# Attention and mixture of experts on one core: the first k and q in two pieces, constants later, products without use at the start, and another order of the attention part

## The chip, the core and the metric

The kernel runs on one NeuronCore of a Trainium2 chip. A core has five engines, each with a queue of its own that it works off in order: PE (TensorE, matrix products, with weight loads that overlap them, PEld), DVE (VectorE), ACT (ScalarE), POOL (GpSimd) and SP (SyncE, which here issues nearly all DMA transfers). Products are written to PSUM, eight banks of 512 float32 a partition, from where ACT or DVE copy them to the core's main memory (SBUF). The metric is the time of one execution in device microseconds; smaller is better.

## The reference

Block-causal attention over 8 batches of 8 heads (576 positions, 64 columns a head, blocks of 64), and behind it a layer of 8 experts, to each of which 576 of the 4608 tokens are assigned greedily by their logits:

```python
scores = scale * np.matmul(q, k.transpose(0, 1, 3, 2))
mask = block_i >= block_j
scores = np.where(mask, scores, -1000000000.0)
attn = np.exp(scores - np.max(scores, axis=-1, keepdims=True))
attn = attn / (np.sum(attn, axis=-1, keepdims=True) + 1e-09)
return np.matmul(attn, v).astype(np.float32)
...
logits = x @ w_gate
order = np.argsort(-logits.flatten())   # greedy, at most N // E tokens an expert
...
for e in range(E):
    h = np.maximum(x[assigned == e] @ w1[e], 0.0)
    out[assigned == e] = h @ w2[e]
```

## The kernel before

The kernel has two stages. The first is attention with the logits (class `Attn`), the second routing and experts (class `Moe`).

Attention works on 32 steps n; a step holds two heads (one in rows 0 to 63 and one in rows 64 to 127), and two steps form a pair u, whose q and k are loaded together. Each float32 q and k is split into two float16 parts (`split`): a cast gives the high part (L277 or L279, on ACT, DVE or POOL), a subtraction the low part (L286). The parts are transposed, for the first four steps on PE (L298, with copies out of PSUM at L306), later by DMA transposes that SP issues (L323), into `qT` and `kT`. `swap` (L336) copies the lower half of kT into the upper half of `kS`, so that two products per block (with kT and with kS) give the scores (L357). A step's scores come in three groups of block rows. For each group DVE finds the row maxima (L375), scales them (L379), and ACT writes the exponentials P (L383). P is transposed on PE with an identity matrix (L427): 25 blocks of 128 x 128 a step, in seven tiles of one PSUM bank each (four blocks, the last one block), in the order of the table PTO; ACT or DVE copies each tile into PT (L408, L410). The value products (L474) read PT and V; DVE scales their result (L444), the result is split again (L454, L458 and L410), and with it the logits are formed (L514) and the rows for the experts are written to device memory (L494, L499). Scores and value products write 64 columns of PE's array, transposes and logits 128; the kernel's own plan calls these shapes N and W.

What sets the order: every task is a Python generator that names its engine (or a choice of engines, as 'AGD'), an estimated duration and the events it needs. `Sched.run` plans with these numbers, picks the next task by start and priority, and writes the instructions of each engine in that order. So a change in a duration, a bias, a priority (the table `PR`, the names PE, PVE, PF) or a limit changes the order of the whole attention stage. Two score buffers ('S', two banks each) and four single banks ('x') are handed out in the plan. Bank 3 is not handed out; products without use write to it.

At the start, `gate` loads w_gate (L227) and scales it, `consts` makes constants for the second stage (L594 to L606 on POOL and DVE), among them the float16 identity `idh` (L598). The first k and q are split in whole halves of nine blocks (step n = 0), four products without use (L283, L301) stand in front and behind the first transposes.

Of the kernel before, what the change touches and what calls it, by code (L numbers as in the profile page):

```python
# [9 lines left out]
F16 = mybir.dt.float16  # L10
# [9 lines left out]
class Sched:  # L20
# [65 lines left out]
    def start(s, k, eng):  # L86
# [73 lines left out]
class Attn:  # L160
# [63 lines left out]
    def gate(s):  # L224
        nc, sc = s.nc, s.sc
        yield S, 25, 'hw'
        nc.sync.dma_start(out=s.wf, in_=s.wg.rearrange("(c p) e -> p c e", p=P))  # L227
        sc.dma(224, ('wg', 0))
        yield D, 100, ('wg', 0)
# [35 lines left out]

    def split(s, nm):
# [3 lines left out]
        for n in range(s.N):  # L270
            u, i = n // 2, n % 2
            yield 'AGD', (573, 760, 760), s.BH, ('ld', nm, n), ('idh', 0), ('tr', nm, 2 * (u - s.NQ) + 1)
# [7 lines left out]
            if n == 0:  # L280

                for _ in range(s.NWU[nm == 'q']):
                    nc.tensor.matmul(s.psb[:, 3], lhsT=s.moe.idh, rhs=b[:, 0:8, hi], start=True, stop=True)  # L283
                sc.free[T] = max(sc.free[T], sc.now) + 427 * s.NWU[nm == 'q']
            yield ('GD', (1300, 780), s.BL) if n else (D, 669)
# [4 lines left out]
            if n < s.NPE:  # L290
                if i == 0:
                    t = s.d[nm + 'T', u] = s.wp.tile([P, 18, P], F16, tag=nm + 'T', name=f"{nm}T{u}", bufs=s.TB)
                yield T, 9 * 107, ('idh', 0), 'x'
# [21 lines left out]
                sc.add(ev(A, 0, 5, ps[0], h=h), 0, sc.now + 200)  # L315
                sc.add(ev(D, 5, 9, ps[1], h=h), 0, sc.now + 200)
# [13 lines left out]
    def swap(s):  # L330

        nc, sc = s.nc, s.sc
        for n in range(s.N):
            u, i = n // 2, n % 2
            yield 'DG', (560, 1280), s.BK, ('tr', 'k', n), ('s', 2 * (u - s.TB) + 1)
            (nc.vector if sc.eng == D else nc.gpsimd).tensor_copy(s.kS[u % s.TB][64:, 9 * i:9 * i + 9], s.d['kT', u][:64, 9 * i:9 * i + 9])  # L336
# [754 lines left out]
```

## Time and profile before

| | us |
|---|---|
| median of 3 runs | 781.56 (781.21 to 783.07) |
| the profiled execution | 781.08 |
| its span, first to last instruction | 779.3 |
| PE busy in the span | 709.6 (91%) |
| DVE busy | 572.2 (73%) |
| ACT busy | 523.3 (67%) |
| POOL busy | 366.1 (47%) |

Engines overlap, so the busy times do not add up to the span. A row of the profile names the source line, the engine, the operation and the tiles; "idle before" is the time its engine waited ahead of it, and the name behind the arrow is what ended that wait. The granted clock (PEclk) is the share of TensorE's full clock.

### The profile page before, as it was taken

How to read it: one execution, taken by the hardware profiler on the slowest of the kernel's cores; microseconds unless marked ns; L12 is line 12 of the kernel's file. 1: busy time of each engine (PE TensorE's matmuls, PEld its weight loads, DVE VectorE, ACT ScalarE, POOL GpSimd, SP SyncE). 2: the span in 40 equal slices, each digit the busy share in tenths (PEclk: the TensorE clock that was granted, in tenths of full speed). 3: DMA queues.
4: the chain of work that ended last, by engine and by line, in shares of the span. 5: the costliest groups of instructions: out<-in, count | busy, mean ns of one | idle time of the engine just before them, and what ended most of it. 6: DMA issues, size and time to landing. Idle time of an engine off the chain costs nothing.

```text
span 779.3 us, 18377 instructions
## 1 busy us (share of the span) xinstructions
PE 709.6 (91%) x6329; PEld 456.0 (59%) x6329; DVE 572.2 (73%) x2299; ACT 523.3 (67%) x1411; POOL 366.1 (47%) x431
## 2 busy tenths in 40 slices
PE   5999999998999999237998999999999999899995
PEld 3676666666677667116546647557475475574752
DVE  6989898888899888887988969778686783520210
ACT  5999987987887876337658497684957847292210
POOL 6785452727263562103244175481944808764001
PEclk9999999999999999658999999999999999999998
DMA  9999999999999997425054192774918439851001
GB/s 194 189 202 187 220 191 193 207 198 221 189 223 169 235 179 188 118 101 178 2 180 159 42 302 58 248 146 149 223 35 254 126 142 236 250 131 42 21 26 36
DMA packets 273485, 124.42 MB, mean 160 GB/s; under 512 B 247280, under 2 KB 256496, under 8 KB 273392
## 3 DMA queue, kind: packets, MB, share of 16 engines
q1 hardware_dynamic: 267504, 104.37, 62.2%
q0 software_dynamic: 5888, 18.88, 7.9%
q8 instruction: 49, 0.80, 0.4%
q14 instruction: 44, 0.36, 0.2%
HBM read 71.32 MB, written 18.87 MB: 116 GB/s over the span
## 4 chain that ended last, share of the span: by engine, by line
PE 75%; DVE 11%; ACT 6%; DMA 4%; issue 3%; POOL 1%; another core or an unknown queue 0%; POOLq 0%; DVEq 0%; SPq 0%; ACTq 0%
PE h L995 23%; PE y L1020 15%; PE psb L427 11%; PE psb L474 10%; PE psb L357 10%; PE y L1024 2%; DVE jk L741 1%; DMA qT<-q 1%; ACT W L914 1%; DVE m L375 1%; ACT raw L910 1%; ACT ja L715 1%; ACT P L383 1%; DVE h L835 1%; DMA kT<-k 1%
## 5 line engine op out<-in xcount | busy, mean ns | idle before, releaser
L995 PE MATMUL h<-X,W 128*128 128x320 f16 (+3 forms) x1536 | 195.5, 287 | 0.3 <-issue 0.3
L995 PEld LDWEIGHTS <-W 128*128 128x128 f16 x1536 | 142.1, 98 | 43.5 <-issue 4.1
L383 ACT ACTIVATE P<-psb,m 128x576 f32<-128x576 f32 (+8 forms) x288 | 149.9, 553 | 22.3 <-DVE m L379 20.5
L1020 PE MATMUL y<-W,HH 128*128 128x512 f16 x512 | 152.2, 379 | 0.0
L375 DVE TENSOR_REDUCE m<-psb 128x1 f32<-128x576 f32 (+8 forms) x288 | 124.6, 480 | 17.0 <-PE psb L357 16.3
L916 POOL TENSOR_TENSOR W<-raw,W 128x1024 f16<-128x1024 f32 x56 | 118.4, 2135 | 37.9 <-ACT W L914 33.4
L427 PE MATMUL psb<-mident,P 128*128 128x128 f32 x800 | 107.6, 280 | 5.5 <-DVE Xf L444 1.7
L474 PE MATMUL psb<-PT,V 128*64 128x448 f32 (+5 forms) x784 | 99.9, 390 | 1.4 <-ACT PT L408 0.7
L981 ACT ACTIVATE HH<-h 128x320 f16<-128x320 f32 (+3 forms) x128 | 52.3, 411 | 70.1 <-PE h L995 61.8
L427 PEld LDWEIGHTS psb<-mident,P 128*128 128x128 f32 x800 | 86.1, 141 | 21.7 <-issue 4.9
L1020 PE MATMUL y<-W,HL 128*128 128x512 f16 x256 | 97.0, 379 | 0.0
L1011 POOL DMA_INDIRECT out_dram<-yo,ix x40 | 39.1, 978 | 118.8 <-ACT yo L1003 86.7
L408 ACT ACTIVATE PT<-psb 128x512 f32<-128x512 f32 (+1 forms) x159 | 81.1, 576 | 15.2 <-PE psb L427 13.6
L357 PE MATMUL psb<-kT,qT 128*64 128x512 f16 (+7 forms) x640 | 86.2, 295 | 2.8 <-DMA qT<-q 2.5
L983 DVE SCALAR_TENSOR_TENSOR HL<-h,HH 128x320 f16<-128x320 f32 (+3 forms) x128 | 56.7, 452 | 43.5 <-ACT HH L981 36.7
L945 POOL DMA_INDIRECT xg<-x,ix x40 | 40.3, 1007 | 98.0 <-DVE ix L883 68.8
L357 PEld LDWEIGHTS <-qT 128*64 128x64 f16 x1280 | 61.3, 111 | 41.1 <-issue 17.6
L357 PE MATMUL psb<-kS,qT 128*64 128x512 f16 (+7 forms) x640 | 78.0, 291 | 0.0
L1020 PEld LDWEIGHTS <-HH 128*128 128x128 f16 x512 | 46.9, 98 | 51.4 <-issue 1.0
L910 ACT ACTIVATE raw<-raw 128x512 f32<-128x512 f32 x112 | 67.7, 627 | 5.7 <-DMA raw<-in_moe_w_dram 5.6
L474 PEld LDWEIGHTS psb<-PT,V 128*64 128x64 f32 x784 | 47.5, 138 | 36.6 <-issue 24.1
L914 ACT ACTIVATE W<-raw 128x512 f16<-128x512 f32 x112 | 68.6, 629 | 0.0
(203 smaller groups left out, 1065.6 us busy)
## 6 DMA issues: line engine op xcount, KB each, us to landing
raw<-in_moe_w_dram SPq DMA_DIRECT2D x64, 512.0 KB
x<-XR SPq DMA_DIRECT2D x8, 1152.0 KB
kn<-in_k_dram SPq DMA_DIRECT2D x15, 576.0 KB
qn<-in_q_dram SPq DMA_DIRECT2D x15, 576.0 KB
V<-in_v_dram SPq DMA_DIRECT2D x64, 128.0 KB
V<-in_v_dram SPq DMA_DIRECT2D x16, 64.0 KB
xg<-x,ix POOLq DMA_INDIRECT x40
out_dram<-yo,ix POOLq DMA_INDIRECT x40
```

The source lines that it names most:

```text
L357: nc.tensor.matmul(ps[64 * h:64 * h + 64, o + a:o + e], lhsT=A[:, h, 64 * i:64 * i + 64], rhs=K[:, h, a:e], start=st, stop=not st)
L375: nc.vector.tensor_reduce(m[:, 0, c:c + 1], ps[:, o:o + 64 * (i + 1)], axis=AX.X, op=OP.max)
L383: nc.scalar.activation(Pt[:, s.OFF[i]:s.OFF[i] + 64 * (i + 1)], ps[:, o:o + 64 * (i + 1)], AF.Exp, bias=m[:, 1, c:c + 1], scale=s.ESC, acc ...
L408: s.nc.scalar.activation(out, in_, AF.Copy)
L427: nc.tensor.transpose(ps[:, a], s.Pb[n % s.NP][:, s.OFF[i] + 128 * j:s.OFF[i] + 128 * j + P], s.ident)
L474: nc.tensor.matmul(ps[64 * h:64 * h + 64, 64 * (i0 - b0):64 * (b1 - b0)], lhsT=vn[:, j, 2 * (n % 2) + h, :], rhs=pt[:, s.PTI[(j, i0)]:s.PT ...
L910: nc.scalar.activation(raw[:,x],raw[:,x],AF.Copy,scale=s.WS)
L914: nc.scalar.activation(hi[:,x],raw[:,x],AF.Copy)
L916: nc.gpsimd.tensor_tensor(lw,raw,hi,op=OP.subtract)
L983: nc.vector.scalar_tensor_tensor(HL[:,f,ts],ps,0.0,HH[:,f,ts],op0=OP.max,op1=OP.subtract)
L995: nc.tensor.matmul(ps,lhsT=W[:,a,d,f*P:f*P+P],rhs=X[:,4*(d//2)+d%2+l,ts],start=(d==0 and n==0),stop=(d==3 and n==2))
L1020: if m<4: nc.tensor.matmul(ps,lhsT=Z[:,f,m*P:m*P+P],rhs=Y[:,a,f],start=(f==n==0),stop=(f==7 and n==2))
```

## The change

The change has these parts:

- The first q and k (step 0) are split in two pieces of five and four blocks (`piece`, new): ACT casts the five, DVE the four, DVE subtracts both; each piece is transposed by itself into one bank. k's upper copy `kS` is written from PSUM by ACT (`twin`, new), no longer from kT by `swap`; kT's pieces and q's second piece are copied by DVE, q's first piece by ACT.
- The load of w_gate stands behind the first loads of k and q; the gate's scaling and the constants on DVE wait, in the plan, for the swap of step 1 (the event `('sw', 1)`). `idh` is made by POOL behind the identity.
- Products without use (`warm`): six at the very front, which read only `idh`, and one behind each of the four pieces' transposes, for the four before.
- Loads get a limit: a load is issued only when the plan holds at most so much transfer time ahead (QL 3000, QV 1000, QW 2500).
- Swaps may also run on ACT; biases, priorities and planner settings are other numbers, and the tiles of P are transposed in ascending order.

```diff
+            if e == 'xx':
+                if len(s.res['x']) < 2:
+                    return None
+                t = max(t, sorted(s.res['x'].values())[1])
+                continue
...
+            if isinstance(e, tuple) and e[0] == 'q':
+                t = max(t, s.q - e[1])
                 continue
...
+        s.sc.free[G] = 5600
...
-        yield S, 25, 'hw'
+        yield S, 25, 'hw', ('gl', 0)
         nc.sync.dma_start(out=s.wf, in_=s.wg.rearrange("(c p) e -> p c e", p=P))
         sc.dma(224, ('wg', 0))
-        yield D, 100, ('wg', 0)
+        yield D, 100, ('wg', 0), ('sw', 1)
...
+    def warm(s, k):
+        for _ in range(k):
+            s.nc.tensor.matmul(s.psb[:, 3], lhsT=s.moe.idh, rhs=s.moe.idh[:, None, :].to_broadcast([P, 4, P]), start=True, stop=True)
+
+    def piece(s, nm, hi, t2, t, c0, c1, e, h):
...
+        yield e, (95 + .835 * w if e == A else 69 + .52 * w), ('ld', nm, 0), ('idh', 0)
...
+        yield D, 69 + 1.042 * w
+        nc.vector.tensor_tensor(b[:, :, 1 - hi], a, b[:, :, hi], op=OP.subtract)
...
+        yield T, 75 * (c1 - c0), 'x'
...
+        for c in range(c0, c1):
+            nc.tensor.transpose(ps[:, c - c0], t2[:, c].rearrange("p a d -> p (a d)"), s.moe.idh)
+        s.warm(s.NW1)
...
+        yield (D, 51 + 83 * (c1 - c0)) if k or c0 else (A, 51 + 110 * (c1 - c0))
...
+    def twin(s, ps, c0, c1, tk, h):
+        yield A, 51 + 110 * (c1 - c0)
+        s.nc.scalar.activation(s.kS[0][64:, c0:c1], ps[:64, :c1 - c0], AF.Copy)
...
+                for c0, c1, e in ((0, 5, A), (5, 9, D)):
+                    sc.add(s.piece(nm, hi, t2, t, c0, c1, e, h), s.PR['split'], sc.now)
...
-            yield 'DG', (560, 1280), s.BK, ('tr', 'k', n), ('s', 2 * (u - s.TB) + 1)
+            yield 'DAG', (560, 1010, 1280), s.BK, ('tr', 'k', n), ('s', 2 * (u - s.TB) + 1)
...
-    PE = 4
-    PVE = 1
+    PE = 2
+    PVE = 2
...
-    BH = 300.0
+    BH = -300.0
...
-    BV = -150.0
+    BV = 150.0
...
-    PTO = (6, 5, 4, 3, 2, 1, 0)
+    PTO = (0, 1, 2, 3, 4, 5, 6)
...
-    PR = dict(load_qk=9, load_v=6, split=3, swap=1, scores=5, transpose=3, values=6, rows=7, logits=5, gate=1)
+    QW = 2500
+    QV = 1000
+    QL = 3000
+    PX = 2
+    PR = dict(load_qk=9, load_v=6, split=3, swap=1, scores=3, transpose=3, values=8, rows=7, logits=5, gate=1)
...
+        s.warm(s.NW0)
+        sc.free[T] = 2000 + 427 * s.NW0
...
+        s.idh=s.cp.tile([P,P],F16,name="m_idh"); nc.gpsimd.tensor_copy(s.idh,s.ident); sc.set(('idh',0))
...
-        yield D,700
-        s.idh=cp.tile([P,P],F16,name="m_idh"); nc.vector.tensor_copy(s.idh,s.ident); s.sc.set(('idh',0))
+        yield D,900,('sw',1)
...
-            sc.ST = 500
+            sc.ST = 100
...
-            sc.KEEP = 0
-            sc.MARGIN = 100
+            sc.MARGIN = 0
+            sc.KEEP = 1
```

DVE at the start of the program, before (the last rows of the constants, the gate, then the first k and q; in these rows `k`, `q` are the split halves, `kn`, `qn` the loaded ones):

```order
L604 TENSOR_SCALAR m_i_136<-m_it 128x32
L605 TENSOR_SCALAR m_b_140<-m_i_136 128x32 x2
L606 TENSOR_SCALAR m_io_144<-m_fi 128x3
L230 TENSOR_SCALAR wgs<-wf 128x4x8
L232 SCALAR_TENSOR_TENSOR wgs<-wf,wgs 128x4x8
L286 TENSOR_TENSOR k_0_156<-kn_128,k_0_156 128x9x64
L286 TENSOR_TENSOR q_0_162<-qn_146,q_0_162 128x9x64
L306 COPY kT_161<-psb 128x512
L336 COPY kS_114<-kT_161 64x1152
L306 COPY qT_166<-psb 128x512
L375 TENSOR_REDUCE m_209<-psb 128x1 x2
```

and the same place now, from its second row on:

```order
L289 CAST k_0_125<-kn_133 128x4x64
L291 TENSOR_TENSOR k_0_125<-kn_133,k_0_125 128x4x64
L291 TENSOR_TENSOR k_0_125<-kn_133,k_0_125 128x5x64
L289 CAST q_0_123<-qn_135 128x4x64
L309 COPY kT_126<-psb 128x512
L291 TENSOR_TENSOR q_0_123<-qn_135,q_0_123 128x5x64
L291 TENSOR_TENSOR q_0_123<-qn_135,q_0_123 128x4x64
L309 COPY kT_126<-psb 128x640
L347 CAST k_0_125<-kn_133 128x9x64
L309 COPY qT_124<-psb 128x512
L347 CAST q_0_123<-qn_135 128x9x64
L442 TENSOR_REDUCE m_201<-psb 128x1 x2
```

The constants and the gate have left this place; pieces of k and q stand there, the copy into kS is gone, and casts of the second halves (step 1, nine blocks) have come in, one of them ahead of qT's copy.

ACT at the same place, before:

```order
L277 ACTIVATE k_0_156<-kn_128 128x9x64
L277 ACTIVATE q_0_162<-qn_146 128x9x64
L306 ACTIVATE kT_161<-psb 128x640
L306 ACTIVATE qT_166<-psb 128x640
L277 ACTIVATE q_0_162<-qn_146 128x9x64
L383 ACTIVATE P_88,m_209<-psb,m_209 128x576
```

and now:

```order
L287 ACTIVATE k_0_125<-kn_133 128x5x64
L287 ACTIVATE q_0_123<-qn_135 128x5x64
L323 ACTIVATE kS_116<-psb 64x512
L323 ACTIVATE kS_116<-psb 64x640
L307 ACTIVATE qT_124<-psb 128x640
L450 ACTIVATE P_90,m_201<-psb,m_201 128x576
```

The two copies into kS have come in, and the cast of q's second half has gone to DVE.

PE in the steady part, before, around one run of transposes of P (`mident` is the identity, `P_88` a step's exponentials); two places 33 rows apart:

```order
L357 LDWEIGHTS qT_584
L357 MATMUL psb<-kS_114,qT_584 64x128
L427 MATMUL psb<-mident,P_88 128x128 x16
L357 LDWEIGHTS qT_584
L357 MATMUL psb<-kT_497,qT_584 64x320
```

```order
L357 MATMUL psb<-kS_114,qT_584 64x64
L427 MATMUL psb<-mident,P_88 128x128 x4
L474 MATMUL psb<-PT_106,V_109 64x448 x4
L357 LDWEIGHTS qT_584
L357 MATMUL psb<-kT_497,qT_584 64x512
```

and one now:

```order
L541 MATMUL psb<-PT_108,V_110 64x64 x2
L541 MATMUL psb<-PT_109,V_110 64x128 x2
L494 MATMUL psb<-mident,P_102 128x128 x25
L422 LDWEIGHTS qT_634
L422 MATMUL psb<-kT_560,qT_634 64x512
```

Before, a step's 25 transposes stand in several runs between scores and value products; now all 25 stand in one, with products of 64 columns on both sides.

More of the change, by code (lines that the diff above doesn't have):

```diff
@@ L247, in load_qk @@
                     sc.dma(1450 * step, ('ld', nm, 2 * u + i))
-                    if u:
+                    if u == i == 0 and nm == 'q':
+                        sc.set(('gl', 0))
+                    if step == 2:
                         sc.ev['ld', nm, 2 * u + 1] = sc.ev['ld', nm, 2 * u]
@@ L264, in load_v, with out @@
             sc.dma(320, ('ld', 'v', u), 625)
+    def warm(s, k):
+        for _ in range(k):
+            s.nc.tensor.matmul(s.psb[:, 3], lhsT=s.moe.idh, rhs=s.moe.idh[:, None, :].to_broadcast([P, 4, P]), start=True, stop=True)
+    def piece(s, nm, hi, t2, t, c0, c1, e, h):
+        nc, sc = s.nc, s.sc
+        w = 64 * (c1 - c0)
+        yield e, (95 + .835 * w if e == A else 69 + .52 * w), ('ld', nm, 0), ('idh', 0)
+        a, b = s.d[nm, 0][:, c0:c1], t2[:, c0:c1]
+        if e == A:
+            nc.scalar.activation(b[:, :, hi], a, AF.Copy)
+        else:
+            nc.vector.tensor_copy(b[:, :, hi], a)
+        yield D, 69 + 1.042 * w
+        nc.vector.tensor_tensor(b[:, :, 1 - hi], a, b[:, :, hi], op=OP.subtract)
+        h.append(-1)
+        if len(h) == 2:
+            sc.set(('sp', nm, 0))
+        yield T, 75 * (c1 - c0), 'x'
+        tk = sc.acq('x')
+        ps = s.bank(tk).bitcast(F16).rearrange("p (c t) -> p c t", t=P)
+        for c in range(c0, c1):
+            nc.tensor.transpose(ps[:, c - c0], t2[:, c].rearrange("p a d -> p (a d)"), s.moe.idh)
+        s.warm(s.NW1)
+        sc.free[T] = max(sc.free[T], sc.now) + 213 * s.NW1
+        k = nm == 'k'
+        if k:
+            sc.add(s.twin(ps, c0, c1, tk, h), s.PR['split'], sc.now + 200)
+        yield (D, 51 + 83 * (c1 - c0)) if k or c0 else (A, 51 + 110 * (c1 - c0))
+        if sc.eng == A:
+            nc.scalar.activation(t[:, c0:c1], ps[:, :c1 - c0], AF.Copy)
+        else:
+            nc.vector.tensor_copy(t[:, c0:c1], ps[:, :c1 - c0])
+        s.out(nm, h, tk)
+    def out(s, nm, h, tk):
+        h.append(tk)
+        if nm == 'q' or h.count(tk) == 2:
+            s.sc.rel('x', tk)
+        if len(h) == (6 if nm == 'k' else 4):
+            s.sc.set(('tr', nm, 0))
+            if nm == 'k':
+                s.sc.set(('sw', 0))
+    def twin(s, ps, c0, c1, tk, h):
+        yield A, 51 + 110 * (c1 - c0)
+        s.nc.scalar.activation(s.kS[0][64:, c0:c1], ps[:64, :c1 - c0], AF.Copy)
+        s.out('k', h, tk)
     def split(s, nm):
@@ L279, in split @@
                 (nc.vector if sc.eng == D else nc.gpsimd).tensor_copy(b[:, :, hi], a)
[L280 to L285, printed above, removed]
+            yield 'GD', (1300, 780), s.BL
             (nc.vector if sc.eng == D else nc.gpsimd).tensor_tensor(b[:, :, 1 - hi], a, b[:, :, hi], op=OP.subtract)
@@ L314, in split @@
                     sc.ev['ti', u] = sc.now
-                sc.add(ev(A, 0, 5, ps[0], h=h), 0, sc.now + 200)
-                sc.add(ev(D, 5, 9, ps[1], h=h), 0, sc.now + 200)
+                sc.add(ev(A, 0, 5, ps[0], h=h), s.PX, sc.now + 200)
+                sc.add(ev(D, 5, 9, ps[1], h=h), s.PX, sc.now + 200)
                 continue
@@ L361, in scores @@
                     sc.set(('s', n))
+                if n == 0:
+                    sc.ev['s1', 0] = sc.now
                 sc.add(s.softmax(n, g, tk, ps), s.PS, sc.now + 200)
@@ L557 @@
     PL = 6
-    PF = 3
+    PF = 5
     NPE = 4
```

36 lines of the change are left out of this document (25 added, 11 removed).

## The prediction

> **What bounds the kernel now.** I read the windows first (per stretch: busy time and count of each engine, granted clock, share of the DMA engines), then the timeline of the first 14 us, then places of PE's timeline, then the groups and the waits.
>
> ```profile
> core 0: us, PE busy (x) PEld busy (x) DVE busy (x) ACT busy (x) POOL busy (x), PEclk, DMA share, GB/s
> 31.00:314.00 283.00, 276.12 (x3016) 191.02 (x3013) 249.55 (x785) 236.42 (x735) 142.00 (x226) 0.99 1.07 200
> 110.00:120.00 10.00, 8.68 (x119) 6.23 (x119) 8.47 (x24) 6.28 (x20) 6.80 (x9) 0.83 1.03 177
> 190.00:200.00 10.00, 7.91 (x73) 5.00 (x74) 6.92 (x23) 4.02 (x13) 5.54 (x5) 0.83 0.94 186
> 314.00:779.30 465.30, 412.68 (x3110) 251.36 (x3110) 298.39 (x1448) 265.54 (x621) 200.46 (x142) 0.95 0.46 133
> ```
>
> Attention ends near 314 us. In its steady part PE is busy 276 of 283 us, DVE 250, ACT 236. The 465 us behind it (routing and experts) hold the same instructions in the same order on every engine in both kernels, so I take them as they are. The whole change is therefore decided ahead of 314 us: before the first scores, and in how PE's stream of scores (L357), transposes of P (L427) and value products (L474) is packed.
>
> **Term 1, the start.** Rows of the timeline: start, duration, what; in brackets the idle time before and who ended it.
>
> ```profile
> 0.73 0.46 SPq L227 DMA_DIRECT2D wf<-in_moe_w_gate_dram  x1
> 1.25 0.49 SPq L245 DMA_DIRECT2D kn<-in_k_dram  x1
> 4.84 0.68 ACT L277 ACTIVATE k<-kn 128x576 f16<-128x576 f32 x1 [2.84 <-DMA kn<-in_k_dram]
> 5.76 0.25 DVE L599 TENSOR_SCALAR m_tri<-m_it 128x128 f16<-128x128 int32 x1 [3.11 <-POOL m_it L594]
> 6.18 0.68 ACT L277 ACTIVATE q<-qn 128x576 f16<-128x576 f32 x1 [0.65 <-DMA qn<-in_q_dram]
> 7.28 0.75 DVE L286 TENSOR_TENSOR k<-kn,k 128x576 f16<-128x576 f32 x1
> 7.57 0.98 POOL L279 CAST k<-kn 128x576 f16<-128x576 f32 x1 [1.53 <-DMA kn<-in_k_dram]
> 7.94 1.22 DVE L286 TENSOR_TENSOR q<-qn,q 128x576 f16<-128x576 f32 x1
> 8.08 1.14 PE L298 MATMUL psb<-m_idh,k 128*128 128x128 f16 x9 [0.59 <-DVE k L286]
> 9.26 0.43 DVE L306 COPY kT<-psb 128x512 f16<-128x512 f16 x1
> 10.64 0.42 DVE L306 COPY qT<-psb 128x512 f16<-128x512 f16 x1
> 11.12 0.20 PEld L357 LDWEIGHTS <-qT 128*64 128x64 f16 x4 [0.28 <-DVE qT L306]
> 12.66 1.29 DVE L375 TENSOR_REDUCE m<-psb 128x1 f32<-128x576 f32 x2 [1.59 <-PE psb L357]
> 13.42 0.68 PE L298 MATMUL psb<-m_idh,k 128*128 128x128 f16 x9
> ...
> L410 DVE CAST XT<-Xf 128x576 f16<-128x576 f32 (+2 forms) x28 | 14.4, 516 | 0.2
> ```
>
> k's high half is cast by 5.52, but its low half starts at 7.28: DVE works through the constants and the gate in between, and those waited for POOL. In the new order they stand later, and k's transfer is issued first. Following DVE's new rows: k is there at 4.84 - 0.52 (issue 0.73 for 1.25) = 4.32, q at 5.66. Cast of four blocks (4/9 of 0.516) to 4.55; both low pieces of k (0.75) to 5.30; wait for q, its cast (0.23) to 5.89; kT copy (0.43) to 6.32; q's low pieces (0.75) to 7.07; kT copy of 640 (0.54) to 7.61; the cast of k's second half, which now stands ahead of qT, to 8.13 (its data came at 7.57 before, 0.5 earlier now); qT copy to 8.55. ACT's new rows end by then too: behind its cast of q's five blocks (5/9 of 0.68, to 6.04) stand copies of 512, 640 and 640 columns, at the 0.68 of 576 columns together 2.1, to 8.2. So scores go on at 8.6 where PE's weights waited until 11.12: 2.5 us. From there PE is still at half rate before (nine transposes take 1.14 at 8.08 and 0.68 at 13.42); the first group runs 11.12 to 12.6, and a group of the same size takes 0.99 later (the pair 291.84 and 292.83 below). With ten products without use from about 2 us on I count it at full rate: 0.5 more. DVE's first reduction moves from 12.66 to about 9.7: **-3.0 us**. The chain of reductions and exponentials that starts there is of the same length, so the gain is carried on. Ends: if q's subtraction stays at 1.22 and the added cast is held up as L336's longest was (0.98, below), -1.5; if ACT's two casts of q that fall away in the next 10 us (0.71 each, L277 below) also shorten it, -4.4. The ten products cost nothing: PE waits for DVE there, and without that cover the last one costs 0.2 to 0.4 (two of its width take 0.41 at 291.84 below). That the pieces bring no earlier start at all is not among my cases, since the constants leave DVE's way in any case.
>
> [...]
>
> **Term 2, changes of shape on PE.** Scores and values write 64 columns of the array, everything else 128. Counted over all of PE's rows of attention, changes between the two fall from 140 to 96, and the 800 transposes of P stand in 41 runs for 77. What one change costs, from four neighbours without a wait:
>
> ```profile
> 289.51 2.40 PE L427 MATMUL psb<-mident,P 128*128 128x128 f32 x20
> 291.84 0.41 PE L357 MATMUL psb<-kT,qT 128*64 128x512 f16 x2
> 292.83 0.33 PE L427 MATMUL psb<-mident,P 128*128 128x128 f32 x1
> 298.27 2.40 PE L427 MATMUL psb<-mident,P 128*128 128x128 f32 x20
> 300.50 0.95 PE L514 MATMUL psb<-wgs,XT 128*128 128x16 f16 x32
> 301.62 0.41 PE L357 MATMUL psb<-kT,qT 128*64 128x512 f16 x2
> 302.52 0.30 PE L357 MATMUL psb<-kT,qT 128*64 128x320 f16 x2
> ```
>
> Twenty transposes take 2.33 to the next start where scores follow and 2.23 where logits (same shape) follow: 0.10. Twelve score products take 0.99 to a transpose and 0.90 to more scores: 0.09. 44 x 0.095 = **-4.2 us**. PE is the busy engine here, so it counts in full, unless a wait takes its place; that is term 3.
>
> **Term 3, longer runs.** Runs of 24 to 26 transposes (a whole head) go from 7 to 28. They need PSUM banks faster than ACT and DVE may empty them:
>
> ```profile
> 92.81 3.03 PE L427 MATMUL psb<-mident,P 128*128 128x128 f32 x25
> 151.11 1.97 PE L427 MATMUL psb<-mident,P 128*128 128x128 f32 x16 [0.80 <-DVE Xf L444]
> 158.31 3.15 PE L427 MATMUL psb<-mident,P 128*128 128x128 f32 x25
> 224.06 3.47 PE L427 MATMUL psb<-mident,P 128*128 128x128 f32 x25
> 230.31 3.10 PE L427 MATMUL psb<-mident,P 128*128 128x128 f32 x25
> 266.69 3.14 PE L427 MATMUL psb<-mident,P 128*128 128x128 f32 x25
> ...
> L427 PE MATMUL psb<-mident,P 128*128 128x128 f32 x800 | 107.6, 280 | 5.5 <-DVE Xf L444 1.7 <-ACT P L383 1.2 <-ACT kT L306 1.1
> ```
>
> Sixteen take 1.97 and twenty 2.40, so 25 without a wait take 2.94. The five whole rows are 0.09 to 0.53 over that, 0.24 on average (the sixth run, broken at 151.11, lost 0.80). 21 more such runs at 0.24 are +5.0. Against it stand the 5.5 us of idle ahead of all 77 runs; with 36 runs fewer I drop 36/77 of it, 2.6. Net **+2.4 us**; ends -0.7 (0.09 each) and +8.5 (0.53 each). I take the mean since five of six rows lie near it.
>
> **Work moved between engines.**
>
> ```profile
> L408 ACT ACTIVATE PT<-psb 128x512 f32<-128x512 f32 (+1 forms) x159 | 81.1, 576 | 15.2 <-PE psb L427 13.6 <-PE psb L514 0.9 <-ACT P L383 0.3
> L410 DVE COPY PT<-psb 128x512 f32<-128x512 f32 (+1 forms) x65 | 39.1, 618 | 0.8 <-PE psb L427 0.5
> L336 DVE COPY kS<-kT 64x1152 f16<-64x1152 f16 x31 | 19.4, 630 | 3.7 <-DMA kT<-k 2.9
> L277 ACT ACTIVATE q<-qn 128x576 f16<-128x576 f32 x27 | 19.3, 714 | 3.9 <-DMA qT<-q 2.1 <-DMA qn<-in_q_dram 1.8
> L279 POOL CAST k<-kn 128x576 f16<-128x576 f32 x13 | 9.8, 752 | 6.0 <-issue 2.7 <-PE psb L298 1.6 <-DMA kn<-in_k_dram 1.5
> ```
>
> Counted from the order: DVE takes 12 casts (0.516) and ten copies of PT (0.618) more and eight swaps (0.630) fewer, +7.4 us; ACT loses 31 casts and ten copies, about -28, and gets some 4 us of small ones; POOL takes 17 casts (0.752), +12.8, and five swaps. DVE goes from 249.6 of 283 to about 257 of 278 (92%). I cost this at nothing: DVE keeps 21 us of idle time and ACT is freed in the same loop. Without that cover it is rival C. Constants and gate, put behind, land in the same idle time.
>
> **Sum.** -3.0 - 4.2 + 2.4 = -4.8 against the profiled execution's 781.1 (span 779.3 and 1.8 around it; the median shown is 0.5 above): **776.3 us**. With the ends of term 1, and term 3 between 0.09 and 0.33 a run (0.33 is the mean with the sixth), 771.8 to 779.7.
>
> **Rivals.** A: *the long runs take the gain back.* Each waits as the worst whole row (0.53): 781.1 - 3.0 - 4.2 + 8.5 = 782.4. For it: DVE's load, and transposes now start with the tile that needs the last exponential of a head. Against: ACT is freer. B: *a wait for transposed q goes too.*
>
> ```profile
> 192.09 0.41 PE L357 MATMUL psb<-kT,qT 128*64 128x512 f16 x2 [2.09 <-DMA qT<-q]
> ...
> SPq L323 <- POOL q L286: 34.6, 11, 6.3
> ...
> L336 DVE COPY kS<-kT x31: 447/454/1434, 9.8 to 282.0; 64x1152 f16<-64x1152 f16 x31
> ```
>
> At 192 us PE idled 2.09 for a DMA transpose, and the clock fell to 0.83 for 10 us (1.7): 3.8 us in one place. If the new issue order of transfers (loads held back while 3 us of transfers are planned ahead) spares it: 772.5. Against: nothing in the order shows that POOL's subtraction, which the transposes wait for (second row: total us, times, longest), ends earlier. C: *DVE becomes the bound by POOL.* L336's copy took 447 ns at least, 454 at the median and 1434 at most (third row); at 0.98 a cast the 12 new ones cost 11.8: 776.3 + 11.8 = 788.1, slower than before. It decides once the delays exceed DVE's 21 us of idle time where PE waits, or fall between a score and its exponential. Against: the mean is 0.63. [...] D: *POOL's added casts make the transposes late*: three more places like 192 us, 776.3 + 11.4 = 787.7; it decides when a pair's last subtraction comes over 2 us later than now.
>
> **Chances.** Forecast 0.54, A 0.16, B 0.15, C 0.07, D 0.08. The range leaves out C and D and gives B some room below: 770 to 784. 0.3% (2.3 us) is about what can be told from no change. Faster by more: most of the forecast (0.46), B, a little of A: 0.64. Within: 0.08 of the forecast and 0.10 of A: 0.18. Slower: C, D and the rest of A: 0.18.
>
> **What would show it.** Term 1: first reduction near 9.7, k's transposes near 5.3 at 0.68 for nine. Term 2: PE's last logits 3 us or more earlier than the start alone explains. Term 3: rows of 25 transposes near 3.2; near 3.5 is A. C: casts of k and q on DVE over 1 us. D: PE waits on qT over 2.5 us in all. A routing and expert part that isn't 465 us would make it all wrong.

## The result, and the profile after

The changed kernel is slower: median 785.18 us of 22 runs beside 778.87 of 22 runs of before on the same chip, a ratio of 1.0077 (95% interval 1.0058 to 1.0095), some 6 us. One of its 22 runs took 1048.75 us at a granted clock of 0.65 and is not in the ratio. Its profiled execution took 784.87 us (span 783.1), the one of before 781.08 (span 779.3).

The windows of the changed kernel: attention now ends at 320 us, not 314, and the part behind it takes 463.1 us beside 465.3. The fourth line is part of the stretch in which most was lost.

```profile
31.00:320.00 289.00, 274.04 (x3008) 194.67 (x3008) 261.79 (x802) 223.53 (x701) 159.50 (x257) 0.99 1.05 196
320.00:783.10 463.10, 412.24 (x3108) 250.42 (x3104) 296.93 (x1445) 264.87 (x621) 200.74 (x142) 0.95 0.46 134
15.00:75.00 60.00, 53.17 (x527) 35.88 (x528) 54.12 (x171) 47.47 (x150) 37.86 (x70) 0.94 0.94 168
46.90:50.30 3.40, 3.40 (x26) 1.66 (x22) 3.27 (x10) 2.04 (x4) 2.74 (x7) 0.50 0.79 136
```

The third stretch in before, which the prediction did not look at: PE, DVE and ACT are all near full there, DVE 55 and ACT 57 of 60 us, and the granted clock is 1.00 throughout.

```profile
15.00:75.00 60.00, 56.71 (x597) 38.98 (x599) 55.28 (x179) 57.10 (x175) 43.15 (x76) 1.00 1.10 195
```

The start in the timeline of the changed kernel (start, duration, what, idle time before):

```profile
1.71 2.74 PE L279 MATMUL psb<-m_idh 128*128 128x512 f16 x6 [1.71 <-POOL m_idh L663]
4.44 0.60 DVE L289 CAST k<-kn 128x256 f16<-128x256 f32 x1 [3.52 <-DMA kn<-in_k_dram]
5.56 0.61 PE L299 MATMUL psb<-m_idh,k 128*128 128x128 f16 x4 [1.11 <-DVE k L291]
8.30 0.74 DVE L347 CAST k<-kn 128x576 f16<-128x576 f32 x1
9.30 0.56 PE L422 MATMUL psb<-kT,qT 128*64 128x512 f16 x2
10.56 1.29 DVE L442 TENSOR_REDUCE m<-psb 128x1 f32<-128x576 f32 x2 [0.49 <-PE psb L422]
```

The first reduction stands at 10.56 beside 12.66: 2.1 us gained.

**Where they are lost.** For every kernel I added up PE's attention products in order of time, each at its streamed columns at the full clock (0.21 us for two of 512 columns side by side, as from 242.78 to 242.99 us in the changed kernel), and noted when a given amount had been started; the table has the lag behind before, in us, negative when ahead. In the same way "last logits" is the start of the last logit product (314.35 us in before). One profiled execution each; the ratio is from all runs beside before on the same chip.

| kernel | 2 us of work | 10 | 22 | 42 | 120 | last logits | ratio (95%) |
|---|---|---|---|---|---|---|---|
| changed | -2.8 | -0.3 | +4.4 | +6.0 | +6.8 | +5.6 | 1.0077 (1.0058 to 1.0095) |
| start_alone | -2.3 | -2.1 | -1.4 | -1.4 | -2.8 | -0.6 | 1.0003 (0.9975 to 1.0031) |
| start_const_late | -2.9 | -2.6 | +3.3 | +4.0 | +4.6 | +6.7 | 1.0074 (1.0044 to 1.0104) |
| no_idle_products | -1.1 | -0.7 | -0.7 | -0.7 | +0.1 | +1.0 | 1.0010 (0.9977 to 1.0043) |
| const_front | -2.2 | +0.3 | +2.5 | +3.9 | +4.5 | +4.0 | 1.0040 (1.0010 to 1.0070) |
| swaps_late | -2.4 | -0.1 | +2.1 | +3.5 | +4.1 | +4.5 | 1.0032 (0.9997 to 1.0067) |
| const_swaps | -2.0 | +0.5 | +2.6 | +3.6 | +4.2 | +5.4 | 1.0040 (1.0013 to 1.0066) |
| long_runs_alone | -1.5 | -1.3 | -1.3 | +0.1 | -0.3 | -1.4 | 0.9981 (0.9952 to 1.0010) |
| long_runs_swaps | -2.3 | -2.2 | -1.8 | -0.4 | +0.3 | +1.4 | 0.9995 (0.9965 to 1.0026) |
| new_ramp_alone | -2.0 | +0.6 | +2.7 | +4.5 | +5.6 | +5.2 | 1.0067 (1.0044 to 1.0090) |
| old_ramp_24 | -1.5 | +1.1 | +1.8 | +3.2 | +4.5 | +2.9 | 1.0025 (0.9998 to 1.0052) |
| old_ramp_40 | -1.5 | -1.3 | +1.2 | +3.8 | +6.5 | +3.7 | 1.0034 (1.0007 to 1.0062) |
| old_ramp_72 | -1.5 | -1.3 | -1.3 | -1.3 | +0.5 | -0.9 | 0.9992 (0.9965 to 1.0019) |
| casts_on_act | -2.7 | -0.2 | +3.6 | +5.0 | +6.4 | +5.6 | 1.0065 (1.0041 to 1.0089) |
| ramp_off_dve | -1.7 | +3.1 | +5.6 | +6.5 | +8.5 | +7.7 | 1.0084 (1.0052 to 1.0117) |
| ramp_no_copies | -2.4 | -0.7 | -0.3 | +0.1 | +2.2 | +1.1 | 1.0020 (0.9997 to 1.0043) |
| writes_behind | -1.7 | -1.5 | -1.4 | -1.4 | -2.6 | +1.8 | 0.9994 (0.9975 to 1.0013) |

The amounts 2, 10, 22, 42 and 120 are reached in before at 16, 31, 44, 67 and 157 us. The changed kernel leads by 2.8 us at 16 us, has given that up by 31 us, is 6 us behind at 67 us, and ends 5.6 behind; between 67 us and the end its lag moves between 3.3 and 9.0. The last logits account for the ratio: 5.6 of 779 us is 0.7%.

What the loss is made of can be read from the windows of one amount of work, from 2 to 42 us of the table. Before, then the changed kernel:

```profile
16.15:67.45 51.30, 48.73 (x527) 33.81 (x523) 47.05 (x157) 48.48 (x152) 37.09 (x69) 1.00 1.12 196
```

```profile
13.35:73.55 60.20, 52.48 (x526) 35.41 (x523) 54.46 (x174) 47.66 (x150) 38.19 (x70) 0.94 0.94 171
```

It takes 8.9 us more. PE's idle time grows from 2.6 to 7.7 us, and the clock falls to half for two stretches of 3.4 us, from 16.1 (granted 0.51 up to 19.5 us) and from 46.9 us (0.50, the fourth line of the first table of windows), each behind a wait of PE (2.42 and 1.62 us): up to 3.4 us more. So PE's waits are some 5 us of the loss, and the clock behind them most of the rest.

The place at 34 to 47 us in the changed kernel's timeline:

```profile
34.16 0.22 DVE L675 TENSOR_SCALAR m_tri<-m_it 128x128 f16<-128x128 int32 x1
35.01 1.33 DVE L678 TENSOR_SCALAR m_bo<-m_i 128x128 f16<-128x128 int32 x1
36.92 0.75 DVE L442 TENSOR_REDUCE m<-psb 128x1 f32<-128x576 f32 x1
38.64 0.74 ACT L450 ACTIVATE P<-psb,m 128x576 f32<-128x576 f32 x1 [2.78 <-DVE m L446]
40.53 1.28 POOL L349 TENSOR_TENSOR k<-kn,k 128x576 f16<-128x576 f32 x1
40.69 2.39 DVE L401 COPY kS<-kT 64x1152 f16<-64x1152 f16 x2
44.43 0.82 DVE L511 SCALAR_TENSOR_TENSOR Xf<-psb,R 128x448 f32<-128x448 f32 x2
45.10 1.49 PE L494 MATMUL psb<-mident,P 128*128 128x128 f32 x9 [1.62 <-DVE Xf L511]
46.53 0.41 PE L422 MATMUL psb<-kT,qT 128*64 128x512 f16 x2
47.95 0.64 PE L422 MATMUL psb<-kT,qT 128*64 128x512 f16 x2
```

The constants hold DVE from 34.16 to 36.92. ACT waits 2.78 us for the maxima behind them. Two copies kS<-kT, 2.39 us, the first beside POOL's subtraction, stand ahead of the next maxima and of Xf, whose bank the run of 25 transposes needs. PE waits, and what follows runs at half rate (two products of 512 columns take 0.64 for 0.41).

### The profile page after: what moved, and what is told of

Same layout as the page of the kernel before. It is cut to its first block, busy times and chain, and to the rows that moved or that the text cites. A ratio compares the mean times of both kernels' runs of the same rounds, so it can differ in the third digit from the quotient of the medians.

```text
span 783.1 us, 18331 instructions
## 1 busy us (share of the span) xinstructions
PE 710.3 (91%) x6335; PEld 460.8 (59%) x6335; DVE 582.1 (74%) x2318; ACT 509.3 (65%) x1379; POOL 379.9 (49%) x449
## 4 chain that ended last, share of the span: by engine, by line
PE 60%; DVE 18%; ACT 9%; DMA 7%; issue 3%; POOL 2%; SPq 0%; POOLq 0%; DVEq 0%; ACTq 0%
PE h L1071 21%; PE y L1096 16%; PE psb L541 7%; PE psb L422 6%; PE psb L494 6%; DVE m L442 5%; ACT P L450 4%; DMA raw<-in_moe_w_dram 4%; PE y L1100 2%; DVE PT L477 2%; DVE jk L817 1%; POOL xg L1021 1%; DMA kT<-k 1%; ACT PT L475 1%; DVE Xf L511 1%
## 5 line engine op out<-in xcount | busy, mean ns | idle before, releaser
L494 PE MATMUL psb<-mident,P 128*128 128x128 f32 x800 | 104.7, 281 | 12.6 <-DVE Xf L511 5.0
L494 PEld LDWEIGHTS psb<-mident,P 128*128 128x128 f32 x800 | 88.1, 142 | 26.8 <-DVE Xf L511 7.7
L541 PE MATMUL psb<-PT,V 128*64 128x448 f32 (+5 forms) x784 | 95.9, 387 | 0.3
L475 ACT ACTIVATE PT<-psb 128x512 f32<-128x512 f32 (+1 forms) x149 | 77.0, 593 | 15.6 <-PE psb L494 13.6
L422 PEld LDWEIGHTS <-qT 128*64 128x64 f16 x1280 | 63.3, 112 | 38.4 <-issue 15.5
```

What stands on the lines that cost most here:

```text
L422: nc.tensor.matmul(ps[64 * h:64 * h + 64, o + a:o + e], lhsT=A[:, h, 64 * i:64 * i + 64], rhs=K[:, h, a:e], start=st, stop=not st)
L475: s.nc.scalar.activation(out, in_, AF.Copy)
L494: nc.tensor.transpose(ps[:, a], s.Pb[n % s.NP][:, s.OFF[i] + 128 * j:s.OFF[i] + 128 * j + P], s.ident)
L541: nc.tensor.matmul(ps[64 * h:64 * h + 64, 64 * (i0 - b0):64 * (b1 - b0)], lhsT=vn[:, j, 2 * (n % 2) + h, :], rhs=pt[:, s.PTI[(j, i0)]:s.PT ...
```

## The experiments

A planner that is given one other number puts the whole order anew, so no experiment plans. A class `Replay` at the end of the changed kernel takes attention's tasks (name, engine, planned time) from a written list, that which before or the changed kernel chose; one edit of the list moves one thing, and every other row of every engine stays where it was. The second stage has the same order in all of them.

```diff
-    sc = Sched()
+    sc = Replay()
```

**The start alone, and the constants' place.** The list of before, with the tasks of the first k and q replaced by the new ones, and `consts` either in front or where the changed kernel has it:

```diff
+ POOL consts (iotas), DVE consts (L675 to L682)     start_alone: ahead of all
  pieces of k and q, twin copies                      from the changed kernel
  ... list of before from step 1 on ...
+ DVE consts (L675 to L682)                           start_const_late: here, in step 2
  DVE reductions of step 2, third group
```

> The new start (pieces, products without use, twin copies) ahead of the order of before: from step 1 on every engine runs what it ran before, in the same order; the seven DVE instructions of the constants stand at DVE's very front, ahead of k's landing. Theory (the start is good for what its first reduction shows, and the new order lost it): the first reduction comes 2.1 us earlier, as in the changed kernel, and the end with it, so about 2 us faster than before (776.8 beside 778.9), the last logits 2 us earlier. Rival (the earlier start puts the engines out of step, and the ramp gives it back whatever the order): no difference to before, within 1 us, with the lead gone by step 4.

> As start_alone, but the constants' seven DVE instructions stand where the changed kernel has them, behind the reductions of step 2 (near 33 us), where DVE is busy all the time. Theory (DVE is what sets the pace there): they cost what they take there, 1.5 to 3 us, so 1.5 to 3 us slower than start_alone. Rival (PE sets the pace, DVE has room): within 0.5 us of start_alone.

(The block is eight instructions; the expectations count the pair of L681 as one.) start_alone keeps a lead of 1.4 us, 2.9 from 115 us on, where before has a slow stretch of the clock (0.83 from 110 to 120 us), until 267 us and loses 2.3 of it by 284 us, most at a wait for a transposed q (below). Its time is that of before: the expected 2 us faster did not come, but neither did a loss. start_const_late goes from 2.6 ahead to 3.3 behind between 36 and 44 us: 5.9 us for 1.8 us of DVE work, where the theory had 1.5 to 3. Its timeline:

```profile
33.61 0.22 DVE L675 TENSOR_SCALAR m_tri<-m_it 128x128 f16<-128x128 int32 x1
35.41 1.47 DVE L401 COPY kS<-kT 64x1152 f16<-64x1152 f16 x1
38.36 0.21 DVE L442 TENSOR_REDUCE m<-psb 128x1 f32<-128x64 f32 x1
38.87 0.53 ACT L450 ACTIVATE P<-psb,m 128x320 f32<-128x320 f32 x1 [4.73 <-DVE m L446]
39.54 1.97 PE L494 MATMUL psb<-mident,P 128*128 128x128 f32 x8 [2.88 <-DVE Xf L511]
```

The block pushed the copy behind it beside POOL's subtraction, where it took 1.47 us; in before the same copy took 0.45:

```profile
36.34 0.45 DVE L336 COPY kS<-kT 64x1152 f16<-64x1152 f16 x1
```

The step's last maxima came at 38.4, ACT stood 4.7 us, PE 2.9, and PE then ran at half rate for 6.8 us. The windows from 2 to 42 us of work, start_alone, then start_const_late with the slow stretch:

```profile
13.85:66.05 52.20, 49.13 (x527) 33.94 (x526) 48.15 (x159) 48.56 (x152) 36.91 (x69) 1.00 1.13 200
```

```profile
13.25:71.45 58.20, 52.12 (x526) 36.05 (x523) 52.22 (x167) 48.70 (x152) 36.20 (x68) 0.94 1.02 187
38.70:45.50 6.80, 5.96 (x31) 4.68 (x32) 5.57 (x19) 5.64 (x18) 5.01 (x8) 0.50 1.04 192
```

PE is idle 3.0 us more, as much as the theory had at most; the other 3 us are the clock, at half for PE's 5.96 busy us. This one move, with what followed it, costs as much as the whole change.

**The products without use.** start_alone with `NW0, NW1 = 0, 0`.

> start_alone without the ten products without use (six ahead of k, one behind each of the four pieces' transposes). The prediction gave 0.5 us of the start to them. Theory (they open the clock a little before the first scores, which in start_alone run at the full rate from 9.30 us): without them the transposes of k and q (0.61 and 0.74 for four and five) stay as they are, the first scores run at half rate, the first reduction comes 0.3 to 0.9 us later (11.0 to 11.4), and the end with it. Rival (the clock had opened by the transposes themselves): no difference, first reduction at 10.5 to 10.6.

start_alone, then no_idle_products:

```profile
6.19 0.40 PE L299 MATMUL psb<-m_idh,k 128*128 128x128 f16 x4 [1.74 <-DVE k L291]
9.13 0.58 PE L422 MATMUL psb<-kT,qT 128*64 128x512 f16 x2
10.41 1.29 DVE L442 TENSOR_REDUCE m<-psb 128x1 f32<-128x576 f32 x2 [1.15 <-PE psb L422]
```

```profile
6.18 1.14 PE L299 MATMUL psb<-m_idh,k 128*128 128x128 f16 x9 [6.18 <-DVE k L291]
9.24 1.03 PE L422 MATMUL psb<-kT,qT 128*64 128x512 f16 x2
11.58 1.29 DVE L442 TENSOR_REDUCE m<-psb 128x1 f32<-128x576 f32 x2 [2.01 <-PE psb L422]
```

Without them everything up to the first scores runs at half rate (k's nine transposes in 1.14 us; nine take 0.68 at 11.17 in start_alone), and the first reduction comes 1.17 us later, more than expected. (The expectation took k's transposes at 0.61 and 0.74 from the changed kernel; in start_alone the first four take 0.40.) The last logits come 1.6 us later; the ratio cannot tell it.

**Constants in front, copies later, both,** in the changed kernel's own order (const_swaps moves only the copies of DVE and ACT, not POOL's):

```diff
+ POOL consts, DVE consts              const_front: ahead of all
...
- DVE consts                           from step 2
...
- DVE swap n                           swaps_late: 24 of 31, each on its own engine
  ... 2 to 28 rows of that engine ...
+ DVE swap n
  PE  scores of step n
```

> The changed kernel, its order kept on every engine, with only the constants' seven DVE instructions and their three iotas moved to the very front, where DVE waits for k. Theory (constants at 34 to 37 us hold up reductions and softmax, and with them the banks): the stalls at 36.0, 40.9 and 46.5 us shrink and 3 to 5 us come back (780 to 782 beside 785.2). Rival A (runs of 25 transposes wait for banks whatever stands on DVE): under 1 us, and the stall of 2.7 us at 40.9 stays.

> The changed kernel, its order kept, with only those copies kS<-kT that stand far ahead of their use (24 of 31) moved later on their own engine's queue, to 1.8 us ahead of the step's first scores by the planned times. Theory (a copy that waits for k's transpose, or that is stretched beside POOL, at the head of DVE's or ACT's queue holds up the Xf and PT copies behind it, and so the banks of the long run): the waits behind runs of 24 and 25 transposes, 18.4 us in all, lose 5 us or more (the ones of 4.1 at 234.7, 2.5 at 192.6, 2.7 at 40.9 and 1.9 at 61.9 us), and the time falls by 3 to 5 us. Rival A (seven banks out of four in one run: the wait is in the run's length): the waits stay within 2 us of 18.4 and the time within 1 us. A third outcome: the copies now stand ahead of the scores, which wait for them, and the time grows.

> The changed kernel with both edits: constants in front, and the copies kS<-kT of DVE and ACT later on their queues (as in long_runs_swaps); nothing of PE's order changed. Theory (these two are the loss): const_front took 0.37% of before's time off the changed kernel's ratio of 1.0077, swaps_late 0.45%; together 4 to 6 us, a ratio of 0.999 to 1.003. Rival (both shortened the same stall near 40 us): no better than the better of the two, 1.003 to 1.004.

const_front gains 1.6 us at the last logits and 0.37% in the ratio, less than expected: the stall at 40 us stays. swaps_late gains 1.2 us and 0.45%. Its waits, beside those of the changed kernel, show why it is no more (total us, times, longest). Changed:

```profile
PE psb L494 <- DVE Xf L511: 5.0, 5, 1.6
PE psb L494 <- DVE PT L477: 3.5, 4, 1.9
```

swaps_late:

```profile
PE psb L494 <- DVE PT L477: 4.1, 4, 1.3
PE psb L422 <- POOL kS L401: 1.3, 3, 0.7
```

The long wait for Xf is gone from this list (0.7 us in all), but waits for PT copies and for the copies themselves took its place. Together the two edits give 1.0040, no better than const_front, as the rival said. That both had shortened the same stall fits the traces: beside the changed kernel, swaps_late has 0.7 us of waits for Xf in all for 5.0, and const_front's at 44 us is 1.21 for 1.62, with a granted clock of 1.00 for 0.84 from 40 to 50 us and still 0.75, beside 0.72, from 14 to 20 us. In const_swaps the wait for Xf at 44 us is gone as well, but waits for PT copies of 1.25 us (at 34.6) and 1.76 us (at 55.3) stand in its place.

**Old and new order, before and behind 60 us.** The list of start_alone up to a planned time (24, 40, 56 or 72 us), behind it that of the changed kernel with the constants in front; new_ramp_alone is the converse. No row is added or lost.

> The order of start_alone (new start, order of before, constants in front) up to step 5, some 56 us by the planned times, and from there the new order of the changed kernel with its whole-step transposition runs: the part of the new order that lies behind the ramp, by itself. Theory (the loss was made between 31 and 70 us; behind that, fewer shape changes and longer waits weigh the same): start_alone kept a lead of 1.4 us on before at that point, so the last logits come 1 to 2.5 us earlier than in before (near 313 beside 314.3) and the time is that of start_alone within 1.5 us. Rival A (each run of 25 waits for banks, by itself): the waits behind these runs, 13.5 us from 70 us on in the changed kernel, cost more than the 32 shape changes saved there (4.8 us), and the last logits come 3 us or more later than start_alone's. The prediction's own terms 2 and 3 would make them about 2 us earlier than start_alone's.

> The converse of long_runs_alone: new start, constants in front, the new order up to 60 us by the planned times (step 5), and from there the order of before with its short runs. Theory (the loss is made in the new order's first 60 us and is kept): behind before by 2 to 4.5 us at 70 us as const_front is (3.9), last logits 317 to 319, ratio 1.003 to 1.005. Rival (the old order behind it takes the loss back, having room that the long runs lack): last logits under 316.

| last logits, lag to before | old order from 60 us | new order from 60 us |
|---|---|---|
| old order up to 60 us | -0.6 (start_alone) | -1.4 (long_runs_alone) |
| new order up to 60 us | +5.2 (new_ramp_alone) | +4.0 (const_front) |

long_runs_alone came out as the theory said, new_ramp_alone somewhat worse (last logits at 319.6 us). The new order's first 60 us cost 5 to 6 us with either order behind them; its runs of 25 transposes behind the ramp cost nothing and gain about 1 us, in single executions.

> As long_runs_alone, with the copies kS<-kT of DVE and ACT (not POOL's) moved later on their queues where they stand over 4 us ahead of the scores, to 2.5 us ahead. Theory (head of DVE's queue): PE's waits for Xf go from about 4 us to under 1.5, those behind long runs by 3 us or more, and the last logits come 2 to 3 us earlier than in long_runs_alone, the fastest of all kernels so far. Rival (another wait takes the place: PT copies, exponentials): under 1 us.

> As long_runs_alone (new start, constants in front, order of before, then that of the changed kernel), but passing to the new order already at 24 us by the planned times, where step 1's scores are done and step 0's transposes are under way. It takes away from const_front only what lies before: PE's stall of 2.4 us at 14 us behind the copies of step 1 and the slow clock after it. Theory (the ramp is lost at three places: 14 to 20 us, 40 us, 60 us): only the first comes back, 1.5 to 2.5 us against const_front, so last logits near 316.3 and a ratio near 1.001 to 1.002. Rival (one early stall shifts everything, and without it the later ones go too): the time of long_runs_alone, last logits near 313.

> The same, passing to the new order at 40 us by the planned times (step 2's transposes begun). Theory: the first two places come back, so 3.5 to 4.5 us against const_front (last logits near 314.3, ratio near 0.9995), and the stall near 60 us stays with its 1.9 us. Rival (the loss is in the passing from one order to the other, or anywhere): no better than old_ramp_24.

> The same, passing at 72 us by the planned times (step 6). Theory: all three places are passed in the old order, which kept a lead of 1.4 us up to here, and the rest weighs the same in both orders: last logits 312 to 313.5, within 1 us of long_runs_alone and of start_alone. If the long runs were a gain of their own (terms 2 and 3 of the prediction, 1.8 us) they would show as 311 to 312; if a loss, as 314 or more.

old_ramp_72 agrees with the theory. old_ramp_24 and old_ramp_40 do not: each lost 2.5 to 3.4 us right behind the point where it passed to the new order, and the stall at 60 us besides. By the expectation's own terms the rival of old_ramp_40 held, no better than old_ramp_24. So there are not three separate places that can be taken out one by one. Two readings are left: wherever steps 1 to 5 run in the new order, the loss is made anew; or a part of it is the price of passing from one order to the other, since long_runs_alone and old_ramp_72 also fall back by some 1.3 us right behind their passing and have won over half of it back by 110 us. const_front and the changed kernel, which pass nowhere, lose all the same, so the passing cannot be all of it. long_runs_swaps missed too: moving the copies cost 2.8 us at the last logits instead of gaining, which its ratio cannot tell.

**DVE's load.** Nine casts from DVE to ACT throughout; six instructions of the first 70 us from DVE to ACT; three copies left out.

```diff
- DVE split cast q/k, steps 4 and later    casts_on_act: the engine alone, 9 tasks
+ ACT split cast q/k
...
- DVE swap 3, 4, 5, 7, cast q 2, 9         ramp_off_dve, on top of const_front
+ ACT swap 3, 4, 5, 7, cast q 2, 9
...
+            if n in (4, 5, 7):              ramp_no_copies, on top of const_front
+                pass
```

> The changed kernel with the nine casts of q and k from step 4 on that it has on DVE (0.74 us each) put on ACT at the same place of the order, as before had nearly all of them. Rival C (DVE became the bound, 7.4 us of work more on it): DVE loses 6.7 us and 3 us or more come back. Theory (DVE's load as such is not it; what stands at the head of its queue at a few places is): within 1.5 us of the changed kernel, a ratio of 1.006 to 1.009.

> const_front with six instructions of the first 70 us put from DVE on ACT at the same place of the order: the casts of q for steps 2 and 9 and the copies kS<-kT of steps 3, 4, 5 and 7 (ACT waits for DVE's maxima there, 1.2 to 1.5 us at a time). PE's order is that of the changed kernel. Theory (DVE has more work than it can do in steps 1 to 5, and the rest of the loss is there): the waits behind the runs at 40 and 60 us, 2.3 and 1.9 us, fall under 1 us each, the lead at 70 us against const_front is 2.5 us or more, last logits near 315.5 beside 318.4 and a ratio of 1.000 to 1.001. Rival (PE's own sequence loses it): under 1 us, ratio 1.003 to 1.004.

> const_front with the copies kS<-kT of steps 4, 5 and 7 left out (those steps multiply by the copies of earlier steps; all of the time's work but these three DVE instructions of 1.4, 1.0 and 1.3 us is kept, in the same order). Theory (DVE has too much to do in steps 1 to 5): the stalls of PE at 40 and 60 us, 2.3 and 1.9 us, fall by half or more, 2 to 4 us come back by 70 us, last logits 314.5 to 316.5 beside 318.4, ratio near 1.000. Rival (PE's own sequence, which asks for a step's seven banks at once before the exponentials and row sums let DVE empty them): under 1 us, 1.003 to 1.004.

casts_on_act changes nothing, against rival C. ramp_off_dve was expected to win and lost 0.4%: in ACT's queue the copies stand ahead of exponentials and PT copies that PE waits for as much, and behind this wait it ran at half rate (four transposes in 1.11 us, for 0.61 at 29.03).

```profile
29.23 1.16 ACT L399 ACTIVATE kS<-kT 64x1152 f16<-64x1152 f16 x1
31.02 0.59 ACT L475 ACTIVATE PT<-psb 128x512 f32<-128x512 f32 x1
31.67 1.11 PE L494 MATMUL psb<-mident,P 128*128 128x128 f32 x4 [2.03 <-ACT PT L475]
```

ramp_no_copies leaves out three copies altogether: with them on no engine, const_front's lag at 42 us of work falls from 3.9 to 0.1 us, for 3.7 us of DVE work. const_front, then ramp_no_copies, where PE waits behind the long runs (the transposes of P stand two lines later in it, at L496):

```profile
44.18 1.49 PE L494 MATMUL psb<-mident,P 128*128 128x128 f32 x9 [1.21 <-DVE Xf L511]
62.62 0.66 PE L494 MATMUL psb<-mident,P 128*128 128x128 f32 x4 [0.64 <-ACT PT L475]
63.86 0.66 PE L494 MATMUL psb<-mident,P 128*128 128x128 f32 x4 [0.58 <-DVE PT L477]
```

```profile
40.78 2.13 PE L496 MATMUL psb<-mident,P 128*128 128x128 f32 x17 [0.31 <-ACT PT L477]
60.05 0.66 PE L496 MATMUL psb<-mident,P 128*128 128x128 f32 x4 [0.38 <-DVE PT L479]
```

About 1 us of the 3.8 is the clock: const_front's scores behind its wait of 2.42 us at 14.7 us ran at half rate, those of ramp_no_copies behind the same wait at full rate (two of 512 columns in 0.64 and 0.41 us). The rest, some 2.8 us, is DVE's work: its time in these steps is paid for by PE. That is not yet why the new order is slower: before makes the copies of steps 4 and 5 near there too, at 36 to 38 us, where they take 0.45 us each, and even without the copies ramp_no_copies is 1.5 us behind start_alone.

**A kernel faster than both?** start_alone with the writes x<-XR of steps 7, 11, 15 and 19 behind the two transposes that follow them on SP.

```diff
- SP rows write x<-XR (L566)
  SP split transpose kT<-k (L382)
  SP split transpose qT<-q (L382)
+ SP rows write x<-XR (L566)
```

> start_alone with four DMAs moved on SP's queue: the writes x<-XR of steps 7, 11, 15 and 19 go behind the transposes of k and q that follow them, instead of ahead. In start_alone the transpose kT<-k behind such a write took 5.9 and 5.7 us (at 176.9 and 259.2) where others took 2.7, the transposed q came late, and PE waited 2.1 us for it twice (188.8 and 271.5 us by the span). Theory (the transpose stands behind the write): these waits go, PE's waits for qT fall from 4.0 to under 1 us, last logits near 310.5 to 312 beside 313.7, ratio 0.995 to 0.998, faster than both kernels. Rival (the transposes wait for POOL's low part of q, not for the write): no change, ratio 0.999 to 1.001.

start_alone's waits and its SP rows, then those of writes_behind:

```profile
PE psb L422 <- DMA qT<-q: 4.0, 2, 2.1
176.86 5.86 SPq L382 DMA_TRANSPOSE kT<-k  x1
```

```profile
PE psb L422 <- ACT P L450: 2.5, 4, 1.7
PE psb L541 <- ACT P L450: 1.9, 1, 1.9
176.54 4.71 SPq L382 DMA_TRANSPOSE kT<-k  x1
```

The waits for q are gone, as expected, though the transpose still takes 4.71 us; waits of the same size for exponentials stand in their place, and the time is the same. No kernel here is measurably faster than before; long_runs_alone (0.9981) comes nearest.

## Why the prediction was wrong

**The step that failed is "Work moved between engines ... I cost this at nothing: DVE keeps 21 us of idle time", with "Constants and gate, put behind, land in the same idle time".** The 21 us were an average over 278 us. From 15 to 75 us of before, where constants, copies and casts were put, DVE was busy 55.3 and ACT 57.1 of 60 us. The constants' place alone cost 5.9 us in the old order, about half of it as half rate behind the waits, and 1.6 in the new; copies of 3.7 us cost about 2.8. Work on an engine that stands between scores and exponentials, and between a bank and its next use, was not free there: it cost from half of its length to three times it.

Put beside the sum: the forecast had -3.0 for the start, 0 for the moved work and -1.8 for terms 2 and 3. Measured were -2.8 at 2 us of work, +8.8 from there to 42 us, and -0.4 from there to the last logits, together +5.6. The place of the +8.8 is shown, the first 60 us of the new order; const_front puts about 2 us of it down to the constants (6.0 to 3.9 at 42 us of work); how the rest divides among the rows is not shown.

**Term 1** was mis-sized: 2.1 us at the first reduction for 3.0. k landed as worked out (4.44 for 4.32), but DVE's cast of its four blocks took 0.60 for the 0.23 reckoned, k's transposes ran at half rate (four in 0.61), and the casts of the second halves took 0.74 each for the 0.516 of the mean row. The full rate at the scores came (the second pair of 512 columns starts 0.24 us behind the first, in no_idle_products 0.42); in start_alone the products without use were worth 1.17 us, where 0.5 was given to them. What decides when the full rate comes is not shown: with the same rows at the same times, k's first four transposes took 0.61 in const_front and 0.40 in ramp_no_copies. "The gain is carried on" held in the old order, not in the new one.

**Terms 2 and 3** had the right sign together, and were off in their parts. Behind the ramp the new order is worth -0.8 us (long_runs_alone beside start_alone) for the -1.8 forecast. Rows of 25 that were not broken by a wait are shorter than forecast (3.18; nine of 17 take 2.95); what is lost instead is lost in a few broken rows, and the idle time ahead of the group is 12.6 us where 5.5 less 2.6 plus 5.0 was reckoned:

```profile
90.83 2.95 PE L494 MATMUL psb<-mident,P 128*128 128x128 f32 x25
L494 PE MATMUL psb<-mident,P 128*128 128x128 f32 x800 | 104.7, 281 | 12.6 <-DVE Xf L511 5.0 <-DVE PT L477 3.5 <-ACT PT L475 2.2
```

**The rivals.** Behind the ramp A falls with these rows and with long_runs_alone; in the ramp the long runs were not tested by themselves, and ramp_no_copies, which keeps them there, is 1.5 us behind start_alone. B's condition came (PE waits 0.3 us for q in the changed kernel), and some of its gain in place: the lag falls from 6.5 us at 186 us to 4.7 at 205. It did not last, since at 235 us two waits for Xf (1.56 and 0.46 us) and a slow stretch (granted clock 0.50 from 238.0 to 241.4 us) cost 4.3 us again. C falls as it was put: casts on DVE took 0.74, not over 1 us, and moving nine of them back gave 0.1%, within noise. But its mechanism was the nearest: DVE instructions, some held up beside POOL (kS<-kT at 1.47 us for 0.45), between a score and its exponential: constants and copies instead of casts. D falls: transposed q was not late. The part behind attention was 463 us, as assumed.

What stays open: which rows of steps 1 to 5 besides the constants and the copies make the new order need more of DVE early on. The loss came back in every variant that kept these steps' order and all their work. Open too is how much of it repeats: the slow stretches of the clock are read from one profiled execution of each kernel, though kernels that share these rows (const_front and new_ramp_alone) agree at 42 us of work within 0.6 us.

## What to carry to other kernels

Before an edit is costed at nothing, read the busy time of the engine that takes it in the very stretch where it will stand: an average over the stage hides a ramp in which nothing is free. On an in-order queue a short instruction costs what it delays, for the engine behind and the one behind that, and a wait that this makes on PE can be followed by a stretch at half clock (0.50 for 6.8 us in start_const_late): 1.8 us of moved constants cost 5.9 us here, half of it in waits and half in the clock. When an order is chosen anew, compare progress (work started against time) with the old one: it shows in one column where the loss was made and where it was only carried along.

## What the runs showed of the hardware

- The same copy kS<-kT (64x1152) took 0.45 us where no subtraction ran on POOL (36.34 in before) and 1.47 where one ran there (35.41 in start_const_late; POOL's subtraction from 35.28 to 36.56). The constant `m_bo` took 0.23 us in start_const_late (34.09, POOL idle) and 1.33 in the changed kernel (35.01; POOL's subtraction from 34.98 to 36.26). What holds DVE up there is not shown.
- In the attention part the granted clock was at half for stretches of 3.4 us (0.50 from 46.9 to 50.3 us in the changed kernel), or of twice that (6.8 in start_const_late). The same wait of PE, 2.42 us, was followed by such a stretch in the changed kernel and in const_front (0.72 and 0.75 on average from 14 to 20 us) and by full rate in ramp_no_copies (1.00), with the same rows ahead of it. const_front, then ramp_no_copies (in ramp_off_dve only the first two products behind this wait ran at full rate, 0.41 us; the next two took 0.57, later ones 0.64):

```profile
17.17 0.64 PE L422 MATMUL psb<-kT,qT 128*64 128x512 f16 x2 [2.42 <-ACT qT L365]
```

```profile
16.98 0.41 PE L424 MATMUL psb<-kT,qT 128*64 128x512 f16 x2 [2.42 <-ACT qT L365]
```

- The part behind the last logits, in one order everywhere, took 460.7 to 473.6 us in the 18 profiled executions, and the median of before was 778.9 to 786.0 us from one set of runs to the next. Single times therefore differ by more than the change is worth. The last logits come ahead of that part: taken from one execution of each kernel, their lag agrees with the ratio of all runs within 2.3 us for all 17.
